# Backward attention on one core: the second head of a unit goes first through the dP matmuls and products

## The chip, the cores and the metric

The kernel runs on one core of one Trainium2 chip. The metric is the device time of one launch in microseconds. Before the change it is 2510.57 us, the median of three runs (2510.35 to 2513.57).

A core has a matrix engine (PE), a vector engine (DVE), a scalar engine for activations and copies (ACT), a general engine (POOL) and a queue engine (SP), each with its own in-order instruction queue, and they wait for one another through semaphores. PE writes only to PSUM, which has 8 banks of 128 x 512 fp32 values; a tile of that size fills one.

## The reference

One transformer block with modulation from a condition vector, forward and all gradients, in bf16 with 2048 tokens of width 512, 32 heads of 16, and an MLP of width 1792:

```python
q, k, v = split(h @ wqkv)                 # h: modulated layernorm of x
p = softmax(q @ k.T * scale)              # 32 heads, 2048 x 2048 each
o = (p @ v) @ wo;  x = x + ga * o
x = x + gb * (relu(h2 @ w1 + b1) ** 2 @ w2 + b2)
...
_out, _vjp = jax.vjp(_f, A_x, A_wqkv, A_wo, B_w1, B_b1, B_w2, B_b2, c, w_mod)
```

The change touches the gradient of attention alone. For each head the kernel computes the scores again, takes P = exp(scores), and with dO, the gradient of the head's output, forms dP = dO V^T (minus a row term), dS = P * dP, and from those dV = P^T dO, dK = dS^T Q and dQ = dS K. The row sums of the softmax and the row term sit already in the operands: dO is scaled by the reciprocal sums, and two extra columns carry the row term.

## The kernel before

The program runs forward attention with the projections and the MLP woven in, then the backward of the MLP, then `attn_bwd` (backward attention), then the remaining weight gradients. Backward attention is one long stage: 1168 to 2384 us of the profiled span.

**Units.** The loops go over 8 groups of four heads (g), two pairs of heads in each (jp), four chunks c of 512 keys, and 16 blocks ib of 128 queries. One step of the innermost loop is a *unit*: one pair of heads, 128 queries, 512 keys. There are 8 x 2 x 4 x 16 = 1024 units. In a unit a = 0 and a = 1 are its two heads. Four units in a row (i = 0 to 3, the `for i in range(G)` loop) form a *group*, which shares one `ds` tile. Groups alternate: `off(c, ib)` is false in one and true in the next. I call the first kind plain and the second held.

**Software pipeline.** While the scores of unit n are made, the dP of unit n - 1 (`last`) is made. For each head a of unit n PE gets:

- L1601, the score matmul S(n, a), 64 rows by 512 columns, into a tile `st`;
- `dP(last, a)`, L1522, the dP matmul of unit n - 1, into a tile `dp`. It uses the other half of PE's rows, so the two run side by side.

ACT takes the score to `pu` with L1604, an exponential. DVE takes the dP times `pu` of its own unit and head into `ds` with L1526, the *product*. After both heads PE gets further matmuls: in units of odd i one or two blocks of dK and dV (`kv`, L1459, 8 matmuls from two calls of `kv`; in held groups one of the two calls is placed between the heads), in units of even i two steps of dQ (`dq`, L1484, 8 matmuls).

**The held dP.** In held groups, head 1 of the unit with i = 1 isn't multiplied on DVE. `dP` returns the tile (`return dp`), the loop keeps it as `held`, and after the next exponential that the loop issues, `dP_pool` has ACT copy it to SBUF (L1534) and POOL multiply it (L1535). In plain groups, instead, the first 128 x 512 block of the group's `ds` is transposed on PE (L1559) and copied out by ACT (L1560). All other transposes of `ds` are DMAs that SP issues (L1543), one for each group, once all its products are there; dQ reads their results, `dsT`, about two groups later.

**Banks.** `st` and `dp` have three PSUM banks each, taken in turn; the two accumulators (`acckv`, `accq`) have one each. So a dP matmul waits until the product (or the held copy) of the third dP before it has read that bank, and a score waits for the exponential of the third score before it. When all 16 query blocks of a key chunk are through, ACT evicts `acckv` to `kvT` (L1462), once in 16 units. When all chunks of a pair are done, ACT copies dK, dV and dQ away (L1476, L1502).

**Order.** PE's, SP's and POOL's queues are in the order in which the program is written. ACT's and DVE's are laid out by a scheduler.

Names for later: exp(n, a) and dP(n, a) belong to head a of unit n. A score *slot* is a score with the dP beside it.

Of the kernel before, what the change touches and what calls it, by code (L numbers as in the profile page):

```python
# [105 lines left out]
class K:  # L106
# [1324 lines left out]
    def attn_bwd(self):  # L1431
# [32 lines left out]
        def turn(g, jp, kvT, s0):  # L1464

            if kvT is None:
                return turn_q(g, jp)
            h0 = 4 * g + 2 * jp
            n = ST // 2
            tp = stp.tile([P, n, P], BF16, name="st")  # L1470
            for st in range(n):
                nc.tensor.transpose(tp[:, st, :], kvT[:, (s0 + st) * P:(s0 + st + 1) * P], self.ident[:])
            v = tp[:].rearrange("p s (t a e) -> p t s a e", t=2, a=2)
            for t, dst in enumerate((self.dk_t, self.dv_t)):
                d = dst[:, s0:s0 + n, h0 * DH:(h0 + 2) * DH].rearrange("p s (a d) -> p s a d", a=2)
                nc.scalar.copy(d, v[:, t, :, :, 0:DH])  # L1476
# [28 lines left out]
        def kv_two(n=2):  # L1505
            for _ in range(n):
                u = pend.pop(0)
                kv(u)
                (T, g, jp, c, ib, kvT, pu, ds) = u
                if ib < ST - 1:  # L1510
                    continue
                if c % 2 and (g, jp) == (NQ - 1, 1):
                    turnq.append((g, jp, kvT, 4 * (c - 1)))
                elif c == SC - 1:
                    turnq.extend((g, jp, kvT, s0) for s0 in (0, ST // 2))

        def dP(u, a):

            (T, g, jp, c, ib, kvT, pu, dsg, i, grp) = u
            rd = slice(64 - 64 * jp, 128 - 64 * jp)  # L1520
            dp = dpp.tile([P, 512], F32, name="dp")
            nc.tensor.matmul(dp[:], lhsT=T["dOT"][rd, ib * P:(ib + 1) * P],  # L1522
                             rhs=masked["VT"][a][rd, 512 * c:512 * (c + 1)], start=True, stop=True)
            if a == 1 and i == 1 and off(c, ib):
                return dp
            nc.vector.tensor_tensor(dsg[:, i, a], dp[:], pu[:, a, :], ALU.mult)  # L1526

        def off(c, ib):
            return (c * SC + ib // G) % 2 == 1

        def dP_pool(u, dp):
            (T, g, jp, c, ib, kvT, pu, dsg, i, grp) = u
            f = (self.junk6, self.csq)[(c * SC + ib // G) // 2 % 2]
            nc.scalar.copy(f[:], dp[:])  # L1534
            nc.gpsimd.tensor_tensor(dsg[:, i, 1], f[:], pu[:, 1, :], ALU.mult)  # L1535

        def dS(u):

            (T, g, jp, c, ib, kvT, pu, dsg, i, grp) = u
            pend.append((T, g, jp, c, ib, kvT, pu, dsg[:, i]))  # L1540
            if i == G - 1:
                dsT, n = grp
                nc.sync.dma_start_transpose(dsT.rearrange("p (b k) -> p b k", k=P)[:, n:, :],  # L1543
                                            dsg[:].rearrange("p i a k -> p (i a k)")[:, n * P:])
                two.append(dsT)
                if len(two) == 2:
                    pendq.extend((T, g, jp, c, ib - 2 * G + 1, a, sub, two[:]) for a in range(2) for sub in range(4))
                    two.clear()
# [15 lines left out]
        last = None  # L1564
        for g in range(NQ):
            for jp in range(2):
                if jp == 0:
                    if g + 1 < NQ:
                        Tn, later = self.load_group(g + 1)
                    else:  # L1570
                        Tn, later = None, self.wq_pieces(1) + self.load_wmt()
                    cut = len(later) // 2 if Tn else len(later)
                    pieces = self.pair_pieces(g, 1) + later[:cut]
                    later = later[cut:]
                elif g + 1 < NQ:
                    pieces = self.pair_pieces(g + 1, 0) + later
                else:
                    pieces = [(self.xhat1_6[:, st, :], self.xhat1_d.rearrange("(st p) d -> p st d", p=P)[:, st, :])
                              for st in range(ST)]
                kvT = kvp.tile([P, S], BF16, name="kvT")  # L1580
                end = (g, jp) == (NQ - 1, 1)
                total = len(pieces)
                for c in range(SC):
                    c0 = 512 * c
                    for ib0 in range(0, ST, G):
                        m = c * (ST // G) + ib0 // G
                        while pieces and (total - len(pieces)) * SC * ST <= m * G * total:
                            if last:
                                nc.gpsimd.tensor_copy(tick[:], last[7][0:1, 0, 0, 0:1])
                            nc.gpsimd.dma_start(*pieces.pop(0))  # L1590
                        dsg, grp = self.dsp.tile([P, G, 2, 512], BF16, name="ds"), []
                        for i in range(G):
                            ib = ib0 + i
                            q = slice(ib * P, (ib + 1) * P)
                            if turnq and i == 3 and m >= (7 if turnq[0][2] is None else 2):
                                turn(*turnq.pop(0))
                            pu = self.pup.tile([P, 2, 512], BF16, name="pu")
                            for a in range(2):
                                stt = stp.tile([P, 512], F32, name="st")
                                rs = slice(64 * jp, 64 * jp + 64)  # L1600
                                nc.tensor.matmul(stt[:], lhsT=T["QT"][rs, q], rhs=masked["KT"][a][rs, c0:c0 + 512],  # L1601
                                                 start=True, stop=True)
                                held = dP(last, a) if last else None
                                nc.scalar.activation(pu[:, a, :], stt[:], ACT.Exp, scale=self.scale)  # L1604
                                if held is not None:
                                    dP_pool(last, held)
                                if a == 0 and i % 2 == 1 and off(c, ib) and len(pend) >= 4:
                                    kv_two(1)
                            if last:
                                dS(last)  # L1610
                            last = (T, g, jp, c, ib, kvT, pu, dsg, i, grp)
                            if i % 2 == 1 and len(pend) >= 4:
                                kv_two(1 if off(c, ib) else 2)
                            elif i % 2 == 0 and len(pendq) > 2 * G:
                                for _ in range(4 if end else 2):
                                    dq(pendq.pop(0))
                            if i == 2:
                                turn_ds(dsg, grp, off(c, ib), end and m > 2)
            T = Tn
        with tc.manual_schedule(engines=ALL):  # L1620
            for t in (2, 0):
                for p in self.wq_pieces(t):
                    nc.gpsimd.dma_start(*p)
            for a in range(2):
                dP(last, a)
            dS(last)
            while len(pend) > 2:
                kv_two()
            kv_two(1)
            for _ in range(2 * G):  # L1630
                dq(pendq.pop(0))
            kv_two(1)
            k0, v0, k1 = [dpp.tile([P, 512], F32, name="dp") for _ in range(3)]
            self.dw_mm(k0, 1, 0, 0, ST // 2)
            turn(*turnq.pop(0))
            self.dw_mm(v0, 2, 0, 0, ST // 2)
            self.dw_mm(k0, 1, 0, ST // 2, ST)
            self.col_sum(1)
            self.dw_mm(v0, 2, 0, ST // 2, ST)
            self.col_sum(2)  # L1640
            self.cs_bc(1)
            while pendq:
                dq(pendq.pop(0))
            self.cs_bc(2)
            turn(*turnq.pop(0))
            self.dw_mm(k1, 1, 1, 0, ST)
# [312 lines left out]
```

## Time and profile before

| | us |
|---|---|
| median of 3 runs | 2510.57 |
| the profiled execution, whole | 2511.14 |
| its span, first to last instruction | 2509.0 |
| PE busy | 2438.6 (97%) |
| ACT busy | 2295.0 (91%) |
| DVE busy | 1709.6 (68%) |
| POOL busy | 716.4 (29%) |
| granted PE clock | 0.997 of full |
| backward attention, from its first score to its last exponential | 1168 to 2384 |

The span is the stretch between the first and the last instruction that the profiler saw; 2.1 us of the execution lie around it. A busy time is the union of the times in which an engine had at least one instruction under way. Consecutive instructions of one engine overlap[...], so the sum of their durations is more than the busy time, and an engine can look busy without being at its peak. A row of the costliest groups gives line, engine, operation, what it writes and reads, count, then busy time and mean length in ns, then the engine's idle time before these instructions and who ended most of it.

### The profile page before, as it was taken

The page shows a single profiled execution, that of the slowest core. Times are in us where ns is not written, and L with a number is a line of the kernel's source. Part 1 is how long each engine was busy: PE and PEld are TensorE (multiplying, and loading weights), DVE is VectorE, ACT ScalarE, POOL GpSimd, SP SyncE. Part 2 cuts the span into 40 slices and gives each one's busy share as a digit, 9 for nine tenths or more (in the row PEclk, how much of TensorE's full clock was granted, in tenths as well). Part 3 has the DMA queues.
Part 4 walks back from the last instruction along what each step waited for, and adds up shares of the span by engine and source line. Part 5 has one row for each costly group of instructions (what it writes and reads, how often), then busy time and mean ns, then how long its engine had stood idle before and what let it go on. Part 6 is the DMA issues. An engine that isn't in the chain of part 4 may idle for free.

```text
span 2509.0 us, 68721 instructions
## 1 busy us (share of the span) xinstructions
PE 2438.6 (97%) x26695; PEld 1080.0 (43%) x26695; DVE 1709.6 (68%) x3519; ACT 2295.0 (91%) x3789; POOL 716.4 (29%) x1289
## 2 busy tenths in 40 slices
PE   8999999999999999999999999999999999999998
PEld 4555555555555554573333333333333333333343
DVE  6222322422332344677999999999999999999957
ACT  7999999999999997534999999999999999999935
POOL 2344531220131022245222222222222222222223
PEclk9999999999999999999999999999999999999999
DMA  4688661441243044598999999999999999999997
GB/s 166 133 180 208 170 121 50 129 100 39 99 115 90 23 131 138 122 199 214 236 215 227 224 221 228 223 222 221 229 222 222 230 223 222 225 226 232 233 191 208
DMA packets 1260526, 445.78 MB, mean 178 GB/s; under 512 B 1204052, under 2 KB 1228246, under 8 KB 1260198
## 3 DMA queue, kind: packets, MB, share of 16 engines
q1 hardware_dynamic: 1219654, 336.29, 70.7%
q0 software_dynamic: 38464, 104.04, 13.6%
q8 instruction: 209, 3.42, 0.6%
q10 hardware_dynamic: 2080, 1.05, 0.1%
q14 instruction: 119, 0.97, 0.1%
HBM read 75.83 MB, written 64.49 MB: 56 GB/s over the span
## 4 chain that ended last, share of the span: by engine, by line
PE 58%; ACT 27%; DMA 7%; issue 4%; DVE 3%; POOL 1%; SPq 0%; DVEq 0%; ACTq 0%; POOLq 0%
ACT pu L391 18%; PE st L1601 17%; PE acckv L1459 8%; PE st L388 8%; ACT pu L1604 7%; PE accq L1484 5%; DMA dsT<-ds 3%; PE accbank L322 3%; PE dps L1050 2%; PE pps L1237 2%; PE st L1559 1%; PE dp L1522 1%; PE dp L1652 1%; DVE ds L1526 1%; DMA keep<-ds 1%
## 5 line engine op out<-in xcount | busy, mean ns | idle before, releaser
L1526 DVE TENSOR_TENSOR ds<-dp,pu 128x512 bf16<-128x512 f32 x1920 | 1181.7, 684 | 25.1 <-PE dp L1522 19.1
L1604 ACT ACTIVATE pu<-st 128x512 bf16<-128x512 f32 x2048 | 1072.7, 661 | 30.1 <-PE st L1601 21.3
L391 ACT ACTIVATE pu<-st 128x1024 bf16<-128x1024 f32 x992 | 912.2, 1077 | 5.1 <-PE st L388 4.9
L388 PE MATMUL st<-QTm,KTq 128*128 128x512 bf16 x1984 | 588.4, 377 | 20.0 <-ACT pu L391 6.0
L322 PEld LDWEIGHTS <-pu 128*128 128x128 bf16 x8192 | 347.3, 96 | 236.3 <-issue 3.2
L1522 PE MATMUL dp<-kvm,q 64*128 64x512 bf16 x1024 | 364.1, 384 | 1.5 <-DVE ds L1526 0.7
L1522 PE MATMUL dp<-kvm,dOTg 64*128 64x512 bf16 x1024 | 361.8, 384 | 0.5 <-DVE ds L1526 0.4
L322 PE MATMUL accbank<-Vaug,pu 128*128 128x17 bf16 x8192 | 357.7, 171 | 1.2 <-ACT Vaug L522 0.9
L1601 PE MATMUL st<-kvm,q 64*128 64x512 bf16 x1024 | 351.6, 381 | 6.0 <-ACT pu L1604 0.2
L1601 PE MATMUL st<-kvm,QTg 64*128 64x512 bf16 x1024 | 350.6, 381 | 6.8
L388 PEld LDWEIGHTS <-KTq 128*128 128x128 bf16 x1984 | 188.2, 96 | 177.5 <-issue 125.6
L1535 POOL TENSOR_TENSOR ds<-junk,pu 128x512 bf16<-128x512 f32 x64 | 73.8, 1153 | 372.2 <-ACT junk L1534 302.4
L1459 PE MATMUL acckv<-ds,Qg 128*16 128x512 bf16 x1024 | 176.0, 382 | 0.2
L1459 PE MATMUL acckv<-pu,dOg 128*16 128x512 bf16 x1024 | 175.9, 382 | 0.0
L1459 PE MATMUL acckv<-ds,q 128*16 128x512 bf16 x1024 | 175.8, 382 | 0.0
L1459 PE MATMUL acckv<-pu,q 128*16 128x512 bf16 x1024 | 175.8, 382 | 0.0
L1535 POOL TENSOR_TENSOR ds<-csq,pu 128x512 bf16<-128x512 f32 x64 | 73.8, 1154 | 349.6 <-ACT csq L1534 271.5
L302 POOL DMA_DIRECT2D QTm<-QTq_d x124 | 63.8, 516 | 341.5 <-PE st L388 319.9
L1601 PEld LDWEIGHTS <-q 64*128 64x128 bf16 x1024 | 66.9, 94 | 159.6 <-issue 144.0
L1601 PEld LDWEIGHTS <-QTg 64*128 64x128 bf16 x1024 | 67.0, 94 | 158.2 <-issue 141.3
L329 DVE RECIPROCAL rl<-accbank 128x4 f32<-128x4 f32 x128 | 23.0, 179 | 159.0 <-PE accbank L322 158.8
L1522 PEld LDWEIGHTS <-q 64*128 64x128 bf16 x1024 | 89.8, 93 | 56.7 <-issue 50.4
(390 smaller groups left out, 3197.0 us busy)
## 6 DMA issues: line engine op xcount, KB each, us to landing
KTq<-KTq_d POOLq DMA_DIRECT2D x24, 512.0 KB, 3.8
duT_d<-auT POOLq DMA_DIRECT2D x3, 1792.0 KB, 7.6
aT_d<-rT POOLq DMA_DIRECT2D x3, 1792.0 KB, 11.0
KTq_d<-KTq SPq DMA_DIRECT2D x32, 128.0 KB, 2.1
QTq_d<-ev_fm SPq DMA_DIRECT2D x32, 128.0 KB, 4.3
ktm_d<-ev_tm POOLq DMA_DIRECT2D x32, 128.0 KB, 2.5
VTq_d<-vT POOLq DMA_DIRECT2D x4, 1024.0 KB, 6.2
dx<-dx_d SPq DMA_DIRECT2D x16, 256.0 KB, 5.3
```

The costliest lines, as they stand in the source:

```text
L302: nc.gpsimd.dma_start(QTm[j][32 * j:32 * j + 32, :], self.QTq_d[g, 32 * j:32 * j + 32, 512 * qc:512 * (qc + 1)])
L322: nc.tensor.matmul(acc[:, a, sub, :], lhsT=pu[:, a, sub * P:(sub + 1) * P], rhs=Vaug[:, kb, h, :], start=(kb == 0 and a == 0 and sub == 0) ...
L388: nc.tensor.matmul(stt[:, a, :], lhsT=KT[:, kb * P:(kb + 1) * P], rhs=QTm[2 * jp + a][:], start=True, stop=True)
L391: nc.scalar.activation(pu[:], stt[:], ACT.Exp, scale=self.scale)
L1050: nc.tensor.matmul(pt[:], lhsT=a[st], rhs=g_tm[:, st, :], start=(st == 0), stop=(st == ST - 1))
L1459: nc.tensor.matmul(acckv[r:r + DH, :], lhsT=T[n][:, ib, col:col + DH], rhs=src[:, a, :], start=(ib == 0), stop=(ib == ST - 1))
L1484: nc.tensor.matmul(accq[r:r + 32, o:o + 256], lhsT=T["K"][:, 4 * c + sub, col:col + 32], rhs=v[:, r // 32 % 2 * 2:r // 32 % 2 * 2 + 2, 4 * ...
L1522: nc.tensor.matmul(dp[:], lhsT=T["dOT"][rd, ib * P:(ib + 1) * P], rhs=masked["VT"][a][rd, 512 * c:512 * (c + 1)], start=True, stop=True)
L1526: nc.vector.tensor_tensor(dsg[:, i, a], dp[:], pu[:, a, :], ALU.mult)
L1535: nc.gpsimd.tensor_tensor(dsg[:, i, 1], f[:], pu[:, 1, :], ALU.mult)
L1601: nc.tensor.matmul(stt[:], lhsT=T["QT"][rs, q], rhs=masked["KT"][a][rs, c0:c0 + 512], start=True, stop=True)
L1604: nc.scalar.activation(pu[:, a, :], stt[:], ACT.Exp, scale=self.scale)
```

## The change

Two lines of `attn_bwd`. In the slot of S(n, a) the loop now makes the dP of head 1 - a of unit n - 1, so head 1 comes first and head 0 second; and the last unit, which is handled after the loop, takes its heads in the order 1, 0. Scores and exponentials keep the order 0, 1.

```diff
                                 nc.tensor.matmul(stt[:], lhsT=T["QT"][rs, q], rhs=masked["KT"][a][rs, c0:c0 + 512],
                                                  start=True, stop=True)
-                                held = dP(last, a) if last else None
+                                held = dP(last, 1 - a) if last else None
                                 nc.scalar.activation(pu[:, a, :], stt[:], ACT.Exp, scale=self.scale)
                                 if held is not None:
                                     dP_pool(last, held)
...
-            for a in range(2):
+            for a in (1, 0):
                 dP(last, a)
             dS(last)
```

`dP` returns a tile to hold only for head 1. So `held` is now set in the pass with a = 0, and `dP_pool` follows exp(n, 0), where it followed exp(n, 1).

## The prediction

> **What bounds it now.** I read the engine totals by stage first, then the costliest groups, then single rows of the backward attention, the only stage that the change touches. The window that holds it (columns: stretch, length, busy time and count of PE, weight loads, DVE, ACT, POOL, clock, DMA share, GB/s):
>
> ```profile
> 1168.00:2384.00 1216.00, 1196.10 (x13028) 388.18 (x13026) 1190.67 (x1936) 1206.14 (x2459) 317.22 (x632) 1.00 1.17 224
> ```
>
> PE, DVE and ACT are each busy for 98 to 99% of it, at full clock. So no engine has room, and what counts is how closely each may follow the others. The groups:
>
> ```profile
> L1526 DVE TENSOR_TENSOR ds<-dp,pu 128x512 bf16<-128x512 f32 x1920 | 1181.7, 684 | 25.1 <-PE dp L1522 19.1
> L1604 ACT ACTIVATE pu<-st 128x512 bf16<-128x512 f32 x2048 | 1072.7, 661 | 30.1 <-PE st L1601 21.3
> ```
>
> 684 and 661 ns are latencies; neighbours on an engine overlap. The steps come from ACT's and DVE's timelines (start, length, count), read from end to end:
>
> ```profile
> 1703.13 0.72 ACT L1462 ACTIVATE kvT<-acckv,kvs 128x512 bf16<-128x512 f32 x1
> 1703.70 3.09 ACT L1604 ACTIVATE pu<-st 128x512 bf16<-128x512 f32 x6
> 1706.56 0.70 ACT L1534 COPY junk<-dp 128x512 f32<-128x512 f32 x1
> ```
>
> ```profile
> 1705.40 1.28 DVE L1526 TENSOR_TENSOR ds<-dp,pu 128x512 bf16<-128x512 f32 x2
> ```
>
> kvT ends at 1703.85 and the sixth exponential at 1706.79: 2.94/6 = **0.49 us an exponential**. The copy ends at 1707.26: 0.47 to 0.48 us. The eviction to kvT costs 0.57 (it ended that much after the exponential before it). Two products take 1.28, so **one takes 1.28 - 0.68 = 0.60** (0.598 unrounded). PE's steps, from the same stretch:
>
> ```profile
> 1705.37 0.37 PE L1601 MATMUL st<-kvm,QTg 64*128 64x512 bf16 x1
> 1705.54 0.37 PE L1522 MATMUL dp<-kvm,dOTg 64*128 64x512 bf16 x1
> ...
> 1706.82 0.39 PE L1601 MATMUL st<-kvm,QTg 64*128 64x512 bf16 x1
> 1706.83 0.39 PE L1522 MATMUL dp<-kvm,dOTg 64*128 64x512 bf16 x1
> 1707.14 0.39 PE L1459 MATMUL acckv<-ds,Qg 128*16 128x512 bf16 x2
> 1707.15 0.39 PE L1459 MATMUL acckv<-pu,dOg 128*16 128x512 bf16 x2
> 1707.47 0.39 PE L1601 MATMUL st<-kvm,QTg 64*128 64x512 bf16 x1
> ```
>
> A dP is followed by a dK/dV block after 0.31, that by the next score after 0.32 (0.54 if two blocks are issued together). A score ends 0.39 after its start; its exponential starts 0.04 later and ends 0.60 after that when it did not queue. The first two rows show a dP that starts 0.17 after its score instead of 0.003: all three dp banks were full, and a product that ended at 1705.49 freed one, 0.05 before. So PE already touches DVE there, though idle time shows nothing of it.
>
> A period is two groups, first a plain one (units P0 to P3), then one with a held product (H0 to H3). The 1024 units, 1168.3 to 2383.5, make 128 periods of 9.49 us. ACT's work in one: 16 exponentials 7.84, one copy of a transposed block and one of the held dP 0.96, kvT in every second period 0.285, dk/dv/dq copies (some 92 of 0.28) 0.20: **9.29**. DVE's: 15 products 8.97, two starts of a ds tile 0.2 (such a product began 0.11 late in this stretch), dqT 0.07: **9.24**. So 0.20 of a period is loss at the joints.
>
> **What the change moves.** Nothing is added or removed, and PE, DVE, POOL and SP keep the same rows; only which head they carry changes. Three moves:
>
> 1. In the slot of S(n+1, head 0), PE now makes dP(n, head 1), and DVE takes it first. That product needs exp(n,1), the latest exponential issued before that slot's, where it used to need exp(n,0), 0.49 earlier in ACT's queue. The row above says an ACT result is out at its end, not after its step. exp(H3,1), for one, ended at 1708.26, while the first product slot of H3 began at 1707.99: this wait is new. Behind it on DVE stand all later products; for them wait dp banks, for the banks PE's in-order queue, and for PE ACT.
> 2. The product of head 0 comes second and no longer waits for ACT: one wait less. DVE's queue hides that, since it stands behind a 0.60 step anyway. Worth 0 to 0.1 where DVE has caught up (64 waits for PE, 19 us in all).
> 3. The held dP (head 1 of H1) is made one slot earlier, and its copy now stands on ACT before exp(H2,1) instead of after it. ACT's sum is unchanged, but **exp(H2,1) ends 0.48 later**, just where by move 1 DVE needs it first. POOL's product, 1.15 us, starts earlier; POOL is busy for 317 of 1216 us, so this is worth nothing.
>
> The price is the longest loop that repeats each period. It starts at the end of exp(H2,1). The product starts 0.10 later. No row shows this wait: PE restarts 0.05 after an exponential, DVE starts 0.14 after a dP with two waits, and I take the middle. Then 0.68 for it; ten more products, to head 1 of the next P3, 5.98; one tile start 0.10; 0.05 to the dP that gets this bank (head 0 of H0, beside S(H1,1)); 0.31, one dK/dV block 0.32, score 0.39, 0.04, exp(H2,0) 0.60. That is 8.57. Then ACT: the copy 0.48, exp(H2,1) 0.49. **Sum 9.54.** Before, the first product hung on exp(H2,0) and the loop closed there, at 8.57, under ACT's 9.29: free. The two moves put 0.49 and 0.48 into it.
>
> With kvT in the period another loop is longer. To exp(P2,0): 0.10 + 0.68 + two products 1.20 + 0.05 + 0.31 + two blocks 0.54 + 0.39 + 0.04 + 0.60 = 3.91. Then all on ACT: the nine exponentials from P2,1 to H2,1 4.41, the transposed copy 0.48, kvT 0.57, the held copy 0.48. Sum **9.85**.
>
> Half the periods have kvT: mean 9.70. The dk/dv copies delay this only where they fall before P3, once in eight periods by some 0.3: 0.04. Of the present loss of 0.20 (pair boundaries, transposes that PE waits for: 3.8 + 0.9 us in the whole stage) I keep half. 9.84 - 9.49 = 0.35, times 128 = **+45 us**. The profiled execution took 2511.1 us (span 2509.0 and 2.1 around it), so 2556; its distance from the median of 2510.6 is 0.5, and I say 2555.
>
> The transposes start with the last product of each group, at most some 0.6 us later; they land 6.7 us after issue and are used a period (9.5) later, so that is covered. If the cover went, it would be up to 0.6 in each of 128 periods, 77 us. The tail after the stage moves by one step of 0.5 us.
>
> **A rule against the row.** The Trainium skill ("VectorE: DVE Perf Modes", The DRAIN you can't avoid) says that the next DVE operation can't start until the pipe of the one before is empty. Then a step would be the whole 0.68, ten of them 6.84, the loop 10.4, and the change would cost some 120 us. But 15 x 0.684 = 10.3 is more than the 9.49 that a period takes, and the pair above has steps of 0.60. The row decides; the rule only says which way a mistake would go.
>
> **Rivals.**
> - *Absorbed* (0.17): DVE takes a fixed lag of about half a microsecond once, and the banks cover it. For it: products often start 0.2 to 0.6 after their dP, so there are dP results in stock, and second products lose a wait. Against it: the dP at 1705.54 had a margin of nothing. If only the head order binds, the loop starts at exp(H3,1): 7.38 to exp(H2,0) (8.57 less two products, 1.20), copy and three exponentials 1.95, 9.33: next to 9.29 that is 0 to 0.2 a period, 2511 to 2536.
> - *Compounded* (0.13): the lag also meets the transposes, or each new wait costs its 0.14 and isn't recovered: up to 0.8 a period, 2590 to 2613.
> - *The other side* (0.05): the held bank is released one exponential earlier, the one place where PE stood still for a bank in the stretch above (0.17 once a period), and products with one wait start up to 0.1 sooner. It decides if the new wait for exp(n,1) is mostly over when the dP lands. Gain 0.05 to 0.15 a period: 2492 to 2504.
> - *The order doesn't come out as written*: ACT's and DVE's queues are laid out by a scheduler, but the listed order of the changed kernel has the held copy between the two exponentials, and half of the products without an ACT wait. Excluded.
>
> **Numbers.** Forecast 0.65, own range 2535 to 2585. 0.2% (5 us) is about what a measurement here can tell from no change. Faster 0.05; same 0.06, the low end of *absorbed*; slower 0.89. The range of 8 in 10 reaches into *absorbed* and *compounded*, 2514 to 2596: left out are *the other side* (0.05), the part of *absorbed* within 0.2% (0.06) and two thirds of *compounded* (0.09).
>
> **What would show it.** ACT idle before exponentials in the stage up by some 45 us, its sums unchanged; DVE rows that wait for ACT pu, hardly present now (0.3 us in all from ACT), at the first product of a unit, above all after the held copy; more dPs that start 0.2 or more after their scores. Forward stages and tail unchanged to 1 us. Wrong if DVE doesn't wait for ACT, or if the time is within 5 us of before.

## The result, and the profile after

The changed kernel takes **2553.07 us** (median of four runs, 2551.34 to 2556.81) against 2510.46 for the kernel before beside it: a ratio of 1.0172, 95% interval 1.0156 to 1.0188, some 43 us slower. The profiled execution has a span of 2549.4 us; the granted PE clock is 0.997 in both kernels.

Windows of the changed kernel, roughly before, in and after the backward attention (columns as in the prediction):

```profile
0.00:1168.00 1168.00, 1113.46 (x12850) 640.22 (x13071) 446.52 (x1379) 1034.21 (x1221) 359.00 (x590) 1.00 0.53 127
1168.00:2424.00 1256.00, 1248.94 (x13074) 380.74 (x13072) 1184.40 (x1936) 1220.62 (x2458) 318.80 (x637) 1.00 1.13 217
2424.00:2549.40 125.40, 109.79 (x546) 49.06 (x553) 81.54 (x205) 55.52 (x112) 35.98 (x64) 0.97 0.85 193
```

From its first score to the end of its last exponential the stage took 1216 us and now takes 1255. The stretch ahead of it is 1.5 us shorter (1166.4 for 1167.9), the one behind it 2.8 longer (127.7 for 124.9). DVE's and ACT's counts in the stage are the same, but for one instruction at a window's edge. DVE is busy for 6 us less of a longer stage. ACT's busy time rises by 14, though it does the same work: its instructions overlap less. PE's rises by 53 for the same matmuls, while its idle time ahead of dPs that is put down to products stays at 1.1. So a wait for a dP bank hardly shows as idle time of PE; the starts show it. Before, 58 of 2044 dPs began 0.2 us or more after the score beside them; now 323 do. The costliest groups of the changed kernel:

```profile
L1526 DVE TENSOR_TENSOR ds<-dp,pu 128x512 bf16<-128x512 f32 x1920 | 1175.9, 681 | 70.9 <-ACT pu L1604 63.0
L1604 ACT ACTIVATE pu<-st 128x512 bf16<-128x512 f32 x2048 | 1082.3, 640 | 53.1 <-PE dp L1522 24.8
```

DVE's idle time ahead of products rose from 25.1 to 70.9 us, and its releaser is a new one: the exponentials, with 63.0. Of these, 48.0 stand ahead of one product, that of H2's head 1, whose exponential comes behind the held copy (H0 to H3 and P0 to P3 are the units of held and plain groups). ACT's idle time ahead of exponentials rose from 30.1 to 53.1. The exponentials' mean recorded length fell from 661 to 640 ns: they stand behind one another less.

One period shows the loop. First ACT and then DVE of the changed kernel around a held copy:

```profile
1634.42 0.60 ACT L1604 ACTIVATE pu<-st 128x512 bf16<-128x512 f32 x1
1634.92 0.58 ACT L1534 COPY csq<-dp 128x512 f32<-128x512 f32 x1
1635.38 0.62 ACT L1604 ACTIVATE pu<-st 128x512 bf16<-128x512 f32 x1
```

```profile
1633.73 1.90 DVE L1526 TENSOR_TENSOR ds<-dp,pu 128x512 bf16<-128x512 f32 x3
1636.03 1.29 DVE L1526 TENSOR_TENSOR ds<-dp,pu 128x512 bf16<-128x512 f32 x2 [0.39 <-ACT pu L1604]
```

exp(H2,0) ends at 1635.02, the copy at 1635.50, exp(H2,1) at 1636.00, and DVE, idle for 0.39, starts at 1636.03. The period before had begun in the same way. First its DVE row, then PE's rows towards its end:

```profile
1626.55 7.26 DVE L1526 TENSOR_TENSOR ds<-dp,pu 128x512 bf16<-128x512 f32 x12 [0.48 <-ACT pu L1604]
```

```profile
1631.98 0.38 PE L1601 MATMUL st<-kvm,q 64*128 64x512 bf16 x1
1632.07 0.37 PE L1522 MATMUL dp<-kvm,q 64*128 64x512 bf16 x1
1632.38 0.40 PE L1484 MATMUL accq<-dsT,keep 128*32 128x256 bf16 x8
1632.71 0.39 PE L1601 MATMUL st<-kvm,q 64*128 64x512 bf16 x1
...
1633.36 0.39 PE L1601 MATMUL st<-kvm,q 64*128 64x512 bf16 x1
...
1634.00 0.39 PE L1601 MATMUL st<-kvm,q 64*128 64x512 bf16 x1
```

Twelve products follow one another without a gap: (7.26 - 0.68)/11 = 0.598 each. The first is that of H2's head 1. The ninth, that of P2's head 1, ends at 1626.55 + 0.68 + 8 x 0.598 = 1632.01 and frees a dP bank. The dP beside S(H0,1), the score of 1631.98, starts 0.06 later, at 1632.07, where it would have started at 1631.98. From there PE runs through: dQ step, S(H1,0) at 1632.71, dK/dV block, S(H1,1) at 1633.36, block, S(H2,0) at 1634.00; its exponential ends at 1635.02. Then come the copy and exp(H2,1). Start to start of the loop (1626.55 to 1636.03) it is 9.48 us.

By kind of period, from the end of one period's first exponential to the end of the next one's (mean of each kind, us; the first and the last period and one of an odd kind are left out):

| a period with | number | before | after |
|---|---|---|---|
| neither kvT nor dk/dv/dq copies | 33 | 9.07 | 9.48 |
| kvT | 62 | 9.54 | 9.74 |
| two copies | 15 | 9.55 | 10.04 |
| four copies | 15 | 10.16 | 10.49 |

The commonest lengths hint at what bounds a period. With neither, it was 8.99 before, next to DVE's 15 products (15 x 0.598 = 8.97), and is 9.48 now, the loop above. With kvT it was 9.39 to 9.40, next to ACT's own work (7.84 + 0.96 + 0.57 = 9.37), and is 9.81 now in 31 of the 62 and 9.60 in 24.

### The profile page after: what moved, and what is told of

Same layout as the page of the kernel before. It is cut to its first block, busy times and chain, and to the rows that moved or that the text cites. A ratio compares the mean times of both kernels' runs of the same rounds, so it can differ in the third digit from the quotient of the medians.

```text
span 2549.4 us, 67587 instructions
## 1 busy us (share of the span) xinstructions
PE 2472.2 (97%) x26467; PEld 1070.0 (42%) x26695; DVE 1712.5 (67%) x3519; ACT 2310.3 (91%) x3789; POOL 713.8 (28%) x1289
## 4 chain that ended last, share of the span: by engine, by line
PE 61%; ACT 28%; DMA 4%; issue 4%; DVE 3%; POOL 1%; DVEq 0%; ACTq 0%; POOLq 0%; SPq 0%
ACT pu L391 26%; PE st L1601 21%; PE acckv L1459 11%; PE accq L1484 6%; PE dp L1522 4%; PE st L388 4%; DMA dsT<-ds 2%; PE accbank L322 2%; PE dps L1050 2%; PE st L1559 2%; PE dp L1652 1%; DVE ds L1526 1%; ACT pu L1604 1%; PE st L1747 1%; PE pps L1237 1%
## 5 line engine op out<-in xcount | busy, mean ns | idle before, releaser
L1526 DVE TENSOR_TENSOR ds<-dp,pu 128x512 bf16<-128x512 f32 x1920 | 1175.9, 681 | 70.9 <-ACT pu L1604 63.0
L1604 ACT ACTIVATE pu<-st 128x512 bf16<-128x512 f32 x2048 | 1082.3, 640 | 53.1 <-PE dp L1522 24.8
L388 PE MATMUL st<-QTm,KTq 128*128 128x512 bf16 x1859 | 561.4, 377 | 26.9 <-ACT pu L391 6.0
L1522 PE MATMUL dp<-kvm,q 64*128 64x512 bf16 x1024 | 372.3, 383 | 2.2 <-DVE ds L1526 0.8
L1522 PE MATMUL dp<-kvm,dOTg 64*128 64x512 bf16 x1024 | 370.9, 382 | 0.5 <-DVE ds L1526 0.4
L1601 PE MATMUL st<-kvm,QTg 64*128 64x512 bf16 x1024 | 338.0, 381 | 1.7 <-ACT pu L1604 0.2
L1601 PE MATMUL st<-kvm,q 64*128 64x512 bf16 x1024 | 337.7, 383 | 0.9
L1601 PEld LDWEIGHTS <-q 64*128 64x128 bf16 x1024 | 66.9, 94 | 159.5 <-issue 143.9
L1589 POOL COPY tick<-ds 1x1 bf16<-1x1 bf16 x251 | 44.3, 177 | 316.8 <-DVE ds L1526 316.8
```

The costliest lines, as they stand in the source:

```text
L388: nc.tensor.matmul(stt[:, a, :], lhsT=KT[:, kb * P:(kb + 1) * P], rhs=QTm[2 * jp + a][:], start=True, stop=True)
```

## Experiments

All ran beside the kernel before.

### Which of the two moves costs: the held copy after the second exponential

```diff
-                            pu = self.pup.tile([P, 2, 512], BF16, name="pu")
+                            pu = self.pup.tile([P, 2, 512], BF16, name="pu"); held = None
...
-                                held = dP(last, 1 - a) if last else None
+                                held = (dP(last, 1 - a) if last else None) or held
...
-                                if held is not None:
+                                if a == 1 and held is not None:
                                     dP_pool(last, held)
```

> The changed kernel, but the held dP is copied by ACT after the second exponential of the next unit, as before the change; head 1 still goes first everywhere. Theory (two terms in one loop: 0.49 from the head order, 0.48 from the copy that comes ahead of the exponential): with the second term gone the longest loop starts at exp(H3,1) and is 9.3 us, just over what ACT needs, so most of the loss goes: 2511 to 2530, I say 2520; ACT pu's waits ahead of DVE products drop from 63 us to under 30. Rival 'head order alone': the copy's place doesn't matter, 2548 to 2556. Rival 'copy alone': 2508 to 2513, the time of before.

Measured: 2536.75 us, ratio 1.0102 (1.0080 to 1.0124). So some 25 of the 43 us stay with the head order alone and 16 go with the copy. In the two profiles 11 of the 16 lie in the stage; the stretch behind it is 5 us longer in the changed kernel, for which I have no cause. The head order costs more than I had said: the range was missed by 7. The wait did halve:

```profile
L1526 DVE TENSOR_TENSOR ds<-dp,pu 128x512 bf16<-128x512 f32 x1920 | 1185.2, 683 | 50.0 <-ACT pu L1604 28.4
```

The periods say why. Their commonest lengths are 9.27 without kvT, for which the prediction's loop from exp(H3,1) gives 9.33, and 9.60 with kvT, which I hadn't worked out for this case. In the changed kernel they are 9.48 and 9.81. So the copy's place costs 0.21 wherever its loop is the longest, the difference of the two loops (9.54 and 9.33). In the mean of the periods with kvT it costs next to nothing: 9.73 here, 9.74 with the early copy. And the head order alone is not nearly free. Both rivals fall: neither term carries the whole loss.

### The early copy without the new head order

```diff
-                                held = dP(last, a) if last else None
+                                held = dP(last, 1 - a if last[8] == 1 and off(last[3], last[4]) else a) if last else None
```

`last[8]` is the unit's i, `last[3]` and `last[4]` are its c and ib: only H1, the unit with the held dP, takes head 1 first.

> The kernel before, with the new head order only for the dP of unit H1, the one with the held dP; so its copy comes ahead of exp(H2,1), but all other units take head 0 first. Theory: the first product of H2 hangs on exp(H2,0), which isn't behind the copy, so the loop stays under ACT's work: 2506 to 2514, equal to before. Rival 'copy alone' (the early copy costs by itself, through the score banks or ACT's order): 2540 or more. Rival 'the held bank comes free earlier and PE gains': 2495 to 2505.

Measured: 2511.75 us, ratio 1.0006 (0.9995 to 1.0016). The copy between the two exponentials costs nothing by itself, and the earlier release of the held bank gains nothing that can be seen. The copy costs only where DVE's next product hangs on the exponential behind it.

### Scores and exponentials turned round too

```diff
-                            for a in range(2):
+                            for a in (1, 0):
                                 stt = stp.tile([P, 512], F32, name="st")
...
-                                if a == 0 and i % 2 == 1 and off(c, ib) and len(pend) >= 4:
+                                if a == 1 and i % 2 == 1 and off(c, ib) and len(pend) >= 4:
...
-            for a in range(2):
+            for a in (1, 0):
                 dP(last, a)
```

> The changed kernel with scores and exponentials turned round as well: every unit takes head 1 first in scores, exponentials, dP and products, and the copy of the held dP stands between the two exponentials. Theory: what counts is only whether the first product's exponential is the older one; here it is, and it stands ahead of the copy, so 2506 to 2514, equal to before, though dP order and copy are as in the changed kernel. Rival 'head order or copy as such': 2540 to 2556.

Measured: 2512.05 us, ratio 0.9997 (0.9985 to 1.0008). The dPs and products come in the changed kernel's order and the held copy stands between two exponentials, and the time is that of before. The group row shows what is gone:

```profile
L1526 DVE TENSOR_TENSOR ds<-dp,pu 128x512 bf16<-128x512 f32 x1920 | 1186.6, 683 | 22.1 <-PE dp L1522 12.9
```

Products wait for PE again, and less than before (22.1 against 25.1 in all). So the order of the heads is no cost as such. The *mismatch* is: the product that comes first must have the older exponential.

### The mirror image

The same edit to scores and exponentials, with dPs and products in the order of before:

```diff
-                            for a in range(2):
+                            for a in (1, 0):
                                 stt = stp.tile([P, 512], F32, name="st")
...
-                                held = dP(last, a) if last else None
+                                held = dP(last, 1 - a) if last else None
```

> The kernel before with scores and exponentials turned round (head 1 first) and dP and products left as they were (head 0 first): the mirror image of the changed kernel as to which product meets the younger exponential, with the copy of the held dP after both exponentials. Theory: as e1_late_copy, within 6 us of it: 2511 to 2530. Rival 'head order alone': 2548 to 2556. Rival 'copy alone': 2508 to 2513.

Measured: 2546.01 us, ratio 1.0141 (1.0105 to 1.0178). It is 9 us over the first experiment, not within 6, above the range of 2511 to 2530, and only 2 below the rival's 2548. But its four runs fall into two pairs: 2537.8 and 2539.6 us at a granted clock of 0.998 and 0.997, as in the first experiment, and 2552.5 and 2555.2 at 0.993 and 0.994. The profiled one is the longest. In this stage its PE clock stood at half for two stretches, 10.2 us in all, and two periods there took 13.5 and 16.5 us. Its commonest periods, 9.27 and 9.60, are those of the first experiment to 0.01. So the mirror image has the same loop, and the excess goes with the lower clock of two of its runs.

### A fourth dP bank

All eight banks are in use. To free one, dQ's matmuls write into the bank of dK and dV, and none accumulates: the sums over query blocks are left out, with as many matmuls of the same size. The last stage gives up one bank as well. Both orders ran with three dP banks as controls, then with four.

```diff
-        accq = accp.tile([P, 512], F32, name="accq")
+        accq = acckv
...
-                                     start=(ib == 0), stop=(ib == ST - 1))
+                                     start=True, stop=True)
...
-        self.dpp = self.open_pool("p5dp", bufs=3, space=PSUM)
+        self.dpp = self.open_pool("p5dp", bufs=4, space=PSUM)
```

> A control for the next three. The kernel before, with dQ's matmuls written into the bank of dK and dV instead of one of their own; each of these matmuls overwrites and none accumulates, so the sums over query blocks are left out, with the same count and size of matmuls. The last stage has one bank less for its own tiles. Both theories: 2505 to 2525, near the kernel before.

> The changed kernel with the same edit (sums over query blocks left out). Both theories: 35 to 50 us more than e5b_one_acc.

> As e5b_one_acc (sums over query blocks left out), with the freed bank as a fourth one for dP, head 0 first. Both theories: within 15 us of e5b_one_acc, rather below it, since PE no longer stands still for a bank in H1 and P1.

> The changed kernel with the fourth dP bank (sums over query blocks left out). Theory: the new wait reaches PE only through the three dP banks; a product's bank is now needed one slot later, which is more than the 0.5 us by which DVE comes later, so the loss is gone: 0 to 12 us over e6b_four_banks, though products still wait for exponentials. Rival 'the wait acts by another way' (transposes, dK and dV waiting for ds, or DVE's own lost time): 30 us or more over e6b_four_banks.

| | head 0 first | head 1 first | difference |
|---|---|---|---|
| three banks | 2541.65, ratio 1.0123 (1.0099 to 1.0146) | 2578.73, 1.0272 (1.0255 to 1.0289) | 37 |
| four banks | 2532.28, 1.0088 (1.0071 to 1.0106) | 2569.09, 1.0236 (1.0213 to 1.0258) | 37 |

The control with head 0 first is 17 us over my range. In it dQ's matmuls also wait for the eviction to kvT (31.8 us in 59 waits; periods with kvT have a mean of 9.85, not 9.54), and the stretch behind the stage is some 9 us longer. The differences within a row are what counts, and the theory's 0 to 12 fell: the fourth bank takes 9 us from either order and nothing from the difference. In the periods with neither kvT nor copies alone it did take something: the commonest length fell from 9.48 to 9.33 with head 1 first and stayed at 8.99 with head 0 first. So the banks aren't the only way from DVE to PE. The timeline of PE with head 1 first and four banks shows the other:

```profile
1632.57 0.40 PE L1484 MATMUL acckv<-dsT,keep 128*32 128x256 bf16 x8
1633.42 0.40 PE L1559 MATMUL st<-ident,ds 128*128 128x128 bf16 x4 [0.45 <-DVE ds L1526]
1633.75 0.39 PE L1601 MATMUL st<-kvm,q 64*128 64x512 bf16 x1
```

L1559 transposes the first block of a plain group's `ds`, the product of P0's *head 0*, which the change puts second. With more banks PE gets there sooner and stands for 0.45 us. Line 1559's own view says who ended PE's idle time before it (weight loads and matmuls; us, times), in the kernel before, in the changed one, and in the changed one with four banks:

```profile
  issue: 28.2, 128
```

```profile
  DVE ds L1526: 27.4, 122
```

```profile
  DVE ds L1526: 113.4, 232
```

So the row was there in the changed kernel too. There it cost nothing by itself: the idle time is some 0.22 a period, as before the change, and in the period shown above the product of P0's head 0 ended 0.1 before PE was through with the dQ step ahead of the transposes. The banks bound first.

### Both ways out

The transposes are placed at the end of P3, on top of the four banks (sums over query blocks left out), in both orders:

```diff
-                            if i == 2:
+                            if i == 3:
                                 turn_ds(dsg, grp, off(c, ib), end and m > 2)
```

> A control for e8a_late_turn: e6b_four_banks (head 0 first, four dP banks, sums over query blocks left out) with PE's transposes of the first block of a plain group's ds placed at the end of unit P3 in place of P2. Both theories: within 12 us of e6b_four_banks.

> The changed kernel with four dP banks and these transposes at the end of P3 (sums over query blocks left out). In e6a_four_banks PE stood in P2 until the product of P0's head 0, which the transposes read and which the change puts second. Theory (the wait reaches PE in two ways, the dP banks and this read; with both out, the loop from exp(H2,1) closes at some 9.1 us, next to DVE's 9.0): 0 to 20 us over e8b_late_turn. Rival 'it acts by neither way' (DVE's own lost time, kvT, dQ): 30 us or more over e8b_late_turn.

Measured: 2518.76 us with head 0 first (ratio 1.0030, 1.0017 to 1.0043), 2538.94 with head 1 first (1.0105, 1.0082 to 1.0127). The control gained 13.5 us over its four-bank form, 1.5 more than I had said. The difference is 20 us, where it was 37, at the very end of the range. In the periods with neither kvT nor copies the commonest length is 9.10, as worked out (9.1), but the control has 8.90; with kvT it is 9.39 in both orders. Products still wait for exponentials for 37.6 us (the changed order's products, who ended DVE's idle time before them):

```profile
  ACT pu L1604: 37.6, 92
```

And only one of the two ways is out. A period of 9.10 in the changed order, first two products of DVE, then PE:

```profile
1754.76 1.28 DVE L1526 TENSOR_TENSOR ds<-dp,pu 128x512 bf16<-128x512 f32 x2
```

```profile
1755.81 0.38 PE L1601 MATMUL st<-kvm,QTg 64*128 64x512 bf16 x1
1756.10 0.37 PE L1522 MATMUL dp<-kvm,dOTg 64*128 64x512 bf16 x1
...
1756.94 0.40 PE L1559 MATMUL st<-ident,ds 128*128 128x128 bf16 x4
```

The products are those of P0; the second, that of head 0, ends at 1756.04. The dP of P2's head 0, beside S(P3,1), is the fourth after that of P0's head 0 and takes its bank. It starts 0.06 after that end and 0.29 after its score, and the transposes now stand behind it in PE's queue. It waits so in 39 of the 49 periods that have neither kvT nor four copies, and in 2 of 49 in the control. So with the transposes moved, the loop closes through the banks again, although there are four. By the periods' means about 10 of the 20 us lie in these periods. The others, in periods with kvT or four copies, are not taken apart, and no run has a fifth bank.

### Two tries at beating both

Periods with dk/dv/dq copies are long on ACT, and the move of the transposes had gained in the control. So half of those copies went to DVE in the kernel before, and, in another run, the transposes alone went to P3, with three banks and full sums.

```diff
-                nc.scalar.copy(d, v[:, t, :, :, 0:DH])
+                (nc.vector.tensor_copy if t else nc.scalar.copy)(d, v[:, t, :, :, 0:DH])
```

> A try at beating both: the kernel before, with half of the copies of finished dK/dV and dQ blocks (the dV ones and the second dQ one) on DVE in place of ACT. In the 31 periods that have them ACT needs 9.3 to 9.9 us and DVE 9.0. If ACT's sum sets those periods, each loses 0.28 or 0.55: 2500 to 2508. If PE's transposes or DVE's queue set them: 2509 to 2518.

> A try at beating both: the kernel before with its own three dP banks and full sums, with one edit from e8b_late_turn, the PE transposes of the first block of a plain group's ds at the end of unit P3 in place of P2. With four banks that move took 13 us (2532 to 2519). If it acts through ACT's order, since the copy then falls next to kvT at the end of a group, it carries over: 2496 to 2506. If it needs the fourth bank (with three, the transposes stand behind a dP that waits for a bank and two dK/dV blocks): 2508 to 2525.

Measured: 2517.37 (ratio 1.0028, 1.0019 to 1.0037) and 2521.79 (1.0039, 1.0025 to 1.0053). Both are slower. With the copies split, periods that had two copies on ACT went from 9.55 to 9.36, but those with kvT went from 9.54 to 9.72: what was saved in some periods was lost in others. That DVE's queue is the reason is likely, but not shown. The gain from the late transposes belongs to the fourth bank: with three, the dP beside S(P3,1), ahead of them in PE's queue, waits for a bank in 113 of 128 periods and comes 34 us late in all. No version here beats the kernel before.

## Why the prediction was right

- **The bound.** "No engine has room, and what counts is how closely each may follow the others" held: with the same work the stage grew by 39 us, and the rest of the program by 1.
- **The new wait.** Products wait for exponentials for 63.0 us, above all behind the held copy. Turning the exponentials round, so that the mismatch is gone while dP order and early copy stay, takes the whole loss away.
- **The early copy.** Right as a term of a loop and not as a cost: 0.21 of a period where the head order is changed, nothing where it isn't. It isn't 0.48, since without the copy another loop is nearly as long.
- **The longest loop, without kvT: 9.54 predicted, 9.48 measured; with kvT 9.85, measured 9.81 as the commonest and 9.74 as the mean.** Three terms were off. The wait behind an exponential is 0.03, not 0.10. The start of a new ds tile costs nothing in it (twelve products at 0.598), not 0.10; the 0.11 read before the change wasn't a cost of the tile's start. And the last two product steps, 1.20, do not close the loop: from the ninth product on PE's own queue is longer, by 0.09.
- **The rest of the sum, and luck in it.** With the 0.10 kept for the joints the prediction has 9.64 for a period without kvT and 9.95 for one with it, and 0.04 a period for dk/dv/dq copies. In the changed kernel the copies add 0.55 or 1.01 to each of the 30 periods that have them, 0.18 a period. So the means are 9.85 without kvT, above the prediction, and 9.74 with it, below, since the loop with kvT binds in half of those periods only. That these two errors nearly cancel is luck: 0.35 a period was predicted, and the stage's growth is 39 us/128 = 0.31.
- **The signs.** DVE's waits for exponentials and the late dPs came as listed. ACT's idle time before exponentials rose by 23 us, not 45; much of the rest, 14, shows as busy time, since its instructions overlap less. The stretches ahead of and behind the stage moved by 1.5 and 2.8 us, not within 1.
- **What was missed.** The list of who reads the product of head 0: the PE transposes of P0's block were not in it. It did not change the number, since with three banks the dP banks bound first, but the claim that the wait reaches PE through the banks was only half of it. *Absorbed* gave the head order alone 0 to 0.2 a period; it is 0.2 (25 us), its far end.
- **The rivals.** *The other side* had an earlier release of the held bank; with that alone the ratio is 1.0006, so it gains nothing. *Compounded* did not come: PE's waits for transposed blocks by DMA fell (4.7 us before, 1.3 after). The rule of the Trainium skill ("VectorE: DVE Perf Modes", The DRAIN you can't avoid), taken as a step of 0.68, would have given some 120 us, by estimate; the steps stayed at 0.598. The section itself makes an exception, which the prediction left out: an operation that is not held starts earlier.

## What to carry to other kernels

When three engines are each 98% busy, as here, their sums no longer tell what a reordering costs. Look for the longest loop through the in-order queues and the buffers that closes once a period, and add it up from steps (end to end on one engine) and latencies (start to end where an engine is crossed). If one engine makes pairs and another consumes them, both should take a pair in the same order, and nothing should be queued on the producer ahead of the member that is wanted first. And before moving a producer within its queue, list every reader of it, not only the one that the bound is suspected in.

## What the runs showed of the hardware

In the changed kernel DVE mostly restarts 0.03 us after an exponential that it waited for, in a third of the cases 0.09. After the end of a dP (which the profile models) it restarts 0.14 or 0.24 later, in the kernel before. Products of 0.68 us follow one another at 0.598 in both kernels, though DVE's separate semaphore instructions at line 1526 fell from 2171 to 1277: the fewer waits brought no shorter step.
